# One list scheduler for all five engines up to block 8 of a chained attention and two-network kernel

## The chip, the cores and the metric

The kernel runs on one core of a Trainium2 chip. The metric is the device time of one execution in microseconds. The core has five engines that run side by side: TensorE (PE, with its weight loads as PEld), VectorE (DVE), ScalarE (ACT), GpSimd (POOL) and SyncE (SP), which here issues nearly all DMAs.

## The reference

All tensors are float32 except that the weights come as float64. Batch 8, 8 heads, 576 positions, head dimension 64; 4608 tokens of width 512 pass through both networks.

```
kv  = einsum('bhsd,bhse->bhde', k, v)
out = einsum('bhsd,bhde->bhse', q, kv)
x   = out / sqrt(mean(out * out, -1) + 1e-6) * g_norm      # to (4608, 512)
h   = max(x @ w1, x @ w2, x @ w3)                          # 512 -> 768
x   = h @ w_out                                            # 768 -> 512
r   = max(x @ w_in, 0)                                     # 512 -> 2048
out = (s * r * r + b) @ w_out2                             # 2048 -> 512
```

## The kernel before, in words

The tokens are cut into nine blocks of 512: blocks 0 to 7 are the first 512 positions of each batch element, block 8 is made of the 64 positions that are left of each of the eight (gathered in `o_rem`). A matrix product in full precision is three passes of PE (`mm3`, lines 95 to 98): each operand is split into a high part of the type fp32r and a low part, made by `split` (lines 91 to 93: ScalarE copies the high part, VectorE or GpSimd subtracts for the low one).

For each block `j` there is attention of batch element `bb` (block 0's own at the start, then that of block `j + 1` beside the products of block `j`), the first product (18 panels `g`, `g1_part`, line 352; `g1_out` takes the maximum of three panels on ScalarE and VectorE, lines 365 and 367) and the second (`g2_mm`, line 373). Attention of one element is four pairs `p` of heads: `load_kv`, `kv_mm` (line 236) into the bank `kvor`, a copy on ScalarE (`kv_out`, for element 0 `kv_diag_pair`, line 251), `q_turn` (line 266), `o_mm` (line 270), `o_out`, and then the norm of each pair: `o_sq`, `sq_split` (line 308), the mean square `ms_mm` into one bank `ms` (line 316; element 0 in the plain form of line 319, which is one matmul in f32, the others as two passes of fp32r), `ms_ln` (three ScalarE steps, lines 328 to 330), `ms_newton` (three VectorE steps, lines 336 to 338; the first is the last reader of `ms`) and `x_split`.

The weights arrive as float64 and are turned into float32 on the core: `conv_unpack` (lines 162 to 167: three ScalarE and three VectorE instructions), `conv_sum` (line 172, GpSimd) and `conv_split`. There are 18 panels for the first product and 6 blocks for the second, all needed within block 0, and three sets of buffers that hold a panel on its way (two while the six blocks are turned). The 32 pieces of the second network's weights are turned during the later blocks and put back to DRAM (`conv_store`).

After block 8 comes the second network (lines 508 on) in Strassen form, on which nothing changes.

What sets the order: each step is put into a list with a position (`at`), one place being one panel of a block (`SL` = 22 places a block; the start has its own scale `US`). `run` (line 68) issues the steps in the order of positions. Up to position 20 SP's queue keeps that order and the other engines are ordered by the framework; from there on PE and SP keep it, and VectorE, ScalarE and GpSimd are ordered by the framework.

## Time and profile before

| | us |
|---|---|
| median of 3 runs (1460.7 to 1464.87) | 1463.11 |
| the profiled execution, its time | 1459.22 |
| its span from the first to the last instruction | 1457.4 |
| PE busy | 1388.7 (95%) |
| VectorE busy | 914.0 (63%) |
| ScalarE busy | 785.8 (54%) |
| GpSimd busy | 319.6 (22%) |
| mean granted TensorE clock | 0.985 |

The shares are means over a span whose stages differ: the start up to about 151 us (block 0, all weights of the first network, attention of elements 0 and 1), blocks 1 to 7 up to 671 us, block 8 up to 736 us, and the second network to the end. The granted clock is a share of 2.4 GHz; half of it is 1.2 GHz. Spans of matmuls overlap, so a row that merges several gives the time that they took together.

### The profile page before, as it was taken

What the parts mean: (1) busy time and instruction counts of PE and PEld (TensorE: products, weight loads), DVE (VectorE), ACT (ScalarE), POOL (GpSimd) and SP (SyncE); (2) the same over time, 40 slices, a digit from 0 to 9 for tenths busy, and PEclk for the clock granted to TensorE, in tenths of its full rate; (3) what the DMA queues carried; (4) which work ended last, traced back from release to release, by engine and by line L of the source; (5) the groups of instructions that cost most, each with busy time, mean ns of one, the idle gap of its engine ahead of it and who ended that gap; (6) DMA issues with size and microseconds to landing.
All of it is one profiled execution on the core that took longest, in us unless ns stands there. A gap on an engine that the chain in (4) does not pass through costs nothing. (4 is left out here: it accounts for less than half of the span.)

```text
span 1457.4 us, 19593 instructions
## 1 busy us (share of the span) xinstructions
PE 1388.7 (95%) x6960; PEld 1127.0 (77%) x6960; DVE 914.0 (63%) x1418; ACT 785.8 (54%) x1389; POOL 319.6 (22%) x238
## 2 busy tenths in 40 slices
PE   5589999898999999999999999999999999999997
PEld 2367777787878787888878878878788888888887
DVE  4996344535353435355476765756777888888785
ACT  5774444435353434443365646646676666656565
POOL 1433232323132323321100000000002414141412
PEclk8789999999999999999999999999999999999999
DMA  9954606172362622213135464453677444454541
GB/s 231 245 167 62 135 22 159 54 158 78 110 125 80 148 87 59 78 31 116 58 130 200 162 230 176 143 202 121 215 261 239 130 151 169 154 170 149 179 135 40
DMA packets 229169, 202.61 MB, mean 139 GB/s; under 512 B 126032, under 2 KB 179280, under 8 KB 226896
## 3 DMA queue, kind: packets, MB, share of 16 engines
q1 hardware_dynamic: 228912, 201.11, 46.6%
q8 instruction: 54, 0.88, 0.3%
q14 instruction: 43, 0.35, 0.1%
q10 hardware_dynamic: 160, 0.26, 0.0%
HBM read 126.88 MB, written 74.45 MB: 138 GB/s over the span
## 5 line engine op out<-in xcount | busy, mean ns | idle before, releaser
L96 PE MATMUL g<-xh,w_w 128*128 128x512 f32 x648 | 258.4, 402 | 6.7 <-ACT xh L92 5.0
L97 PE MATMUL g<-xl,w_w 128*128 128x512 f32 x648 | 255.6, 394 | 0.1
L98 PE MATMUL g<-xh,w_w 128*128 128x512 f32 x648 | 255.1, 394 | 0.0
L92 ACT ACTIVATE zx<-z 128x512 fp32r<-128x512 f32 (+1 forms) x280 | 161.2, 586 | 123.2 <-PE zs_a L710 35.3
L632 PE MATMUL ps_a<-x_q,w_q 128*128 128x512 f32 (+1 forms) x960 | 211.2, 371 | 3.0 <-DVE cs L540 2.6
L710 PE MATMUL zs_a<-zx,w_q 128*128 128x512 f32 (+1 forms) x960 | 203.7, 369 | 0.5 <-POOL zx L93 0.3
L632 PEld LDWEIGHTS ps_a<-x_q,w_q 128*128 128x128 f32 x960 | 167.1, 188 | 38.6 <-DVE cs L540 5.8
L93 POOL TENSOR_TENSOR zx<-z,zx 128x512 fp32r<-128x512 f32 (+1 forms) x46 | 63.6, 1383 | 594.1 <-DMA gd<-cs 382.2
L93 DVE TENSOR_TENSOR zx<-z,zx 128x512 fp32r<-128x512 f32 (+1 forms) x234 | 171.9, 752 | 34.8 <-ACT zx L92 34.4
L710 PEld LDWEIGHTS zs_a<-zx,w_q 128*128 128x128 f32 x960 | 167.8, 188 | 31.9 <-POOL zx L93 0.7
L96 PEld LDWEIGHTS g<-xh,w_w 128*128 128x128 f32 x648 | 124.1, 192 | 37.8 <-ACT xh L92 6.6
L98 PEld LDWEIGHTS g<-xh,w_w 128*128 128x128 f32 x648 | 123.2, 190 | 26.4
L97 PEld LDWEIGHTS g<-xl,w_w 128*128 128x128 f32 x648 | 123.2, 190 | 26.3 <-POOL xl L93 0.8
L172 POOL TENSOR_TENSOR tr_ctr<-tr_ctr,gc_cgc 128x512 int32<-128x512 int32 x42 | 56.2, 1337 | 263.6 <-DVE gc_cgc L167 179.2
L162 DVE TENSOR_SCALAR gc_cgc<-raw_craw 128x512 uint16<-128x512 uint16 x42 | 19.9, 475 | 144.6 <-DMA raw_craw<-in_moe_w_in_dram 70.3
L632 PE MATMUL ps_b<-x_q,w_q 128*128 128x512 f32 (+1 forms) x480 | 107.6, 372 | 1.4 <-ACT cs L643 0.8
L710 PE MATMUL zs_b<-zx,w_q 128*128 128x512 f32 (+1 forms) x480 | 103.7, 370 | 2.1 <-DVE zx L93 2.1
L367 DVE TENSOR_TENSOR h<-g,h 128x512 f32<-128x512 f32 x108 | 73.8, 683 | 42.4 <-PE g L98 42.0
L632 PEld LDWEIGHTS ps_b<-x_q,w_q 128*128 128x128 f32 x480 | 83.8, 188 | 19.3 <-ACT cs L643 1.6
L710 PEld LDWEIGHTS zs_b<-zx,w_q 128*128 128x128 f32 x480 | 83.9, 188 | 18.9 <-DVE zx L93 3.3
L163 ACT ACTIVATE tr_ctr<-raw_craw 128x512 int32<-128x512 uint32 x42 | 28.0, 667 | 118.2 <-DMA wd<-tr_ctr 99.0
L96 PE MATMUL g<-h,w_o 128*128 128x512 f32 x216 | 84.1, 390 | 0.6 <-DVE h L367 0.6
(158 smaller groups left out, 2216.7 us busy)
## 6 DMA issues: line engine op xcount, KB each, us to landing
z<-gd SPq DMA_DIRECT2D x64, 512.0 KB
gd<-cs SPq DMA_DIRECT2D x96, 256.0 KB
z<-gd SPq DMA_DIRECT2D x48, 256.0 KB
x1d<-x SPq DMA_DIRECT2D x36, 256.0 KB
raw_craw<-in_moe_w_in_dram SPq DMA_DIRECT2D x16, 512.0 KB
wd<-tr_ctr SPq DMA_DIRECT2D x32, 256.0 KB
raw_craw<-in_moe_w_out_dram SPq DMA_DIRECT2D x64, 128.0 KB
gd<-d SPq DMA_DIRECT2D x32, 256.0 KB
```

What stands on the lines that cost most here:

```text
L92: act(out=hi, in_=src, func=AF.Copy)
L93: eng.tensor_tensor(out=lo, in0=src, in1=hi.bitcast(F32), op=ALU.subtract)
L96: nc.tensor.matmul(ps, lhsT=w[:, 0, sl], rhs=xh, start=first, stop=False)
L97: nc.tensor.matmul(ps, lhsT=w[:, 0, sl], rhs=xl, start=False, stop=False)
L98: nc.tensor.matmul(ps, lhsT=w[:, 1, sl], rhs=xh, start=False, stop=last)
L162: ts(out=c, in0=w16[:, :, 3], scalar1=0x7FFF, scalar2=None, op0=ALU.bitwise_and)
L163: act(out=r, in_=w32[:, :, 0], func=AF.Copy, scale=2.0 ** -29)
L172: nc.gpsimd.tensor_tensor(out=t, in0=t, in1=g.bitcast(I32), op=ALU.add)
L367: nc.vector.tensor_tensor(out=st["h", m], in0=ps, in1=st["h", m], op=ALU.max)
L632: nc.tensor.matmul(ps, lhsT=w[:, a, c], rhs=x[:, b_], start=new and k == 0 and e == 0, stop=k == HK - 1 and e == 2, skip_group_check=True)
L710: nc.tensor.matmul(ps, lhsT=w[:, a, c], rhs=x[:, b_, :n], start=new and k_ == 0 and e == 0, stop=k_ == 3 and e == 2, skip_group_check=True)
```

## The change

Every step up to position `CUT` (just ahead of block 8) becomes a `job` with its engine, a duration in us, and the names that it reads (`r`), writes (`w`) and allocates (`a`). `arrange` builds the dependences from these names and from the number of buffers of each tag (`SIZE`), and then plays the engines in time: whenever an engine is free it takes, of the jobs that are ready, the one with the lowest position. A VectorE job that begins while a GpSimd job runs is charged 0.9 us more; a job of SP is followed by 2.0 us until its data are there. The jobs are issued in the order of their begin, and within that region all five engines keep that order. Jobs from `CUT` on join the list of before.

The steps that held several instructions are cut into jobs of one each (`conv_unpack` becomes `conv_c`, `conv_r`, `conv_t`, `conv_m`, `conv_g`; `ms_ln` becomes `rsqrt`, `ms_newton` becomes `newton`, each split a high and a low job). Positions at the start are new. Element 0 goes through the same `kvc` and `rps` tiles as the others (`kvf` and its copies of half a diagonal go), all four pairs of its keys and values have `k` and `v` tiles (two had tiles of the tag `o`), and element 1 takes its mean squares in the plain form too (`PLAIN = 2`). In blocks 0 and 1's input the low parts are made by VectorE (before: two of four pairs of each by GpSimd). For elements 2 to 7 the keys and values of the pairs are loaded 3 places apart from 16 places ahead of the block (before: from 5.9 places ahead and 1 apart for elements 4 to 7, earlier for 2 and 3).

The core of the diff:

```diff
-    plan = []
+    plan, jobs = [], []
+    SIZE = {"g": 4, "t": 2, "st": 2, "qt": 2, "o": 2, "kvc": 3, "k": NP, "v": NP}
     def at(pos, fn, *args):
         plan.append((pos, len(plan), fn, args))
+    def job(pos, eng, cost, fn, *args, r=(), w=(), a=()):
+        jobs.append((pos, len(jobs), eng, cost, fn, args, r, w, a))
+    def arrange(todo):
+        writer, readers, users, owner, rings, need, after = {}, {}, {}, {}, {}, [], [[] for _ in todo]
+        for n, e in enumerate(todo):
+            owner.update((nm, n) for _, nm in e[8])
+            for nm in {key.split(":")[0] for key in (*e[6], *e[7])} | {nm for _, nm in e[8]}:
+                users.setdefault(nm, []).append(n)
+        for n, (_, _, eng, cost, fn, args, r, w, a) in enumerate(todo):
+            deps = set()
+            for tag, nm in a:
+                past = rings.setdefault(tag, [])
+                if past:
+                    deps.add((past[-1][0], False))
+                if len(past) >= SIZE.get(tag, 1):
+                    deps.update((m, True) for m in users[past[-SIZE.get(tag, 1)][1]])
+                past.append((n, nm))
+            for key in (*r, *w):
+                if key in writer:
+                    deps.add((writer[key], True))
+                if owner.get(key.split(":")[0], n) != n:
+                    deps.add((owner[key.split(":")[0]], False))
+            for key in w:
+                deps.update((m, True) for m in readers.pop(key, ()))
+                writer[key] = n
+            for key in r:
+                readers.setdefault(key, []).append(n)
+            deps = {d for d in deps if d[0] != n}
+            need.append(len(deps))
+            for m, full in deps:
+                after[m].append((n, full))
+        free, ready, heaps, out, pool = {}, [0.0] * len(todo), {}, [], 0.0
+        for n, e in enumerate(todo):
+            if not need[n]:
+                heaps.setdefault(e[2], []).append(n)
+        while any(heaps.values()):
+            begin, eng = min((max(free.get(e, 0.0), min(ready[n] for n in h)), e) for e, h in heaps.items() if h)
+            n = min(m for m in heaps[eng] if ready[m] <= begin)
+            heaps[eng].remove(n)
+            cost = todo[n][3]
+            if eng == "DVE" and begin < pool:
+                cost += 0.9
+            free[eng] = begin + cost
+            if eng == "POOL":
+                pool = begin + cost
+            end = begin + cost + (2.0 if eng == "SP" else 0.1)
+            out.append((begin, n))
+            for m, full in after[n]:
+                ready[m] = max(ready[m], end if full else begin)
+                need[m] -= 1
+                if not need[m]:
+                    heaps.setdefault(todo[m][2], []).append(m)
+        assert len(out) == len(todo)
+        return [todo[n] for _, n in out]
     def run():
-        todo = sorted(plan, key=lambda e: e[:2])
-        n = sum(e[0] < 20 for e in todo)
-        with tc.manual_schedule(engines={EngineType.SP}):
-            for _, _, fn, args in todo[:n]:
-                fn(*args)
+        order = sorted(jobs, key=lambda e: e[:2])
+        n = sum(e[0] < CUT for e in order)
+        with tc.manual_schedule(engines={EngineType.PE, EngineType.SP, EngineType.DVE, EngineType.Activation, EngineType.Pool}):
+            for e in arrange(order[:n]):
+                e[4](*e[5])
+        todo = sorted(plan + [(e[0], e[1] - len(jobs), e[4], e[5]) for e in order[n:]], key=lambda e: e[:2])
         with tc.manual_schedule(engines={EngineType.PE, EngineType.SP}):
-            for _, _, fn, args in todo[n:]:
+            for _, _, fn, args in todo:
                 fn(*args)
...
     def load_kv(bb, p):
-        kv = None if bb or p < 2 else at_.tile([P, 2, 2, C, D], F32, tag="o", bufs=NP // 2, name=f"kv_{p}")
-        for i, (nm, src) in enumerate((("k", k), ("v", v))):
-            t = st[nm, bb, p] = (at_.tile([P, 2, C, D], F32, tag=nm, bufs=NP, name=f"{nm}_{bb}_{p}")
-                                 if kv is None else kv[:, i])
+        for nm, src in (("k", k), ("v", v)):
+            t = st[nm, bb, p] = at_.tile([P, 2, C, D], F32, tag=nm, bufs=NP, name=f"{nm}_{bb}_{p}")
...
     def ms_mm(bb, p):
         ps = st["ms", p] = psa.tile([P, N], F32, tag="ms", name=f"ms_{bb}_{p}")
-        if bb == 0:
+        if bb < PLAIN:
             nc.tensor.matmul(ps, lhsT=onesf, rhs=st["sq", p], start=True, stop=True)
             return
...
+    def plan_conv(kk, src, pos, load, a, pr, gc, slot=None, store=None):
+        key = (kk[0], int(kk[1:]))
+        raw, tr, g = f"raw_{kk}", f"tr_{kk}", f"gc_{kk}"
+        c = g + "c:c" if gc == "st" else g + ":c"
+        ra, tra, gca = stage(a, pr, gc)
+        job(load, "SP", 2.23, conv_load, key, src, ra, w=[raw], a=[(a, raw)])
+        job(pos, "DVE", 0.43, conv_c, key, gca, r=[raw], w=[c], a=[(gc, g)] + ([(gc, g + "c")] if gc == "st" else []))
+        job(pos, "ACT", 0.67, conv_r, key, tra, r=[raw], w=[tr + ":r"], a=[(pr, tr)])
+        for i in range(2):
+            job(pos, "ACT", 0.71, conv_t, key, i, r=[c], w=[tr + ":t"])
+        job(pos, "DVE", 0.69, conv_m, key, r=[raw], w=[tr + ":r"])
+        job(pos, "DVE", 0.69, conv_g, key, r=[raw, tr + ":r"], w=[g + ":g"])
+        job(pos, "POOL", 1.35, conv_sum, key, r=[g + ":g"], w=[tr + ":t"])
+        if slot:
+            job(pos, "ACT", 0.63, conv_hi, key, slot, r=[tr + ":t"], w=[f"W_{kk}:0"], a=[(slot, f"W_{kk}")])
+            job(pos, "DVE", 0.69, conv_lo, key, r=[tr + ":t", f"W_{kk}:0"], w=[f"W_{kk}:1"])
+        else:
+            job(store, "SP", 1.1, conv_store, key, r=[tr + ":t"])
+    def plan_kv(bb, load, mm, n):
+        job(load(0) + 0.01, "SP", 1.1, load_rem, bb, w=["rem"])
         for p in range(NP):
...
+            job(load(p), "SP", 2.5, load_kv, bb, p, w=[f"k{bb}.{p}", f"v{bb}.{p}"],
+                a=[("k", f"k{bb}.{p}"), ("v", f"v{bb}.{p}")])
+            job(mm(p), "PE", 0.65, kv_mm, bb, p, r=[f"k{bb}.{p}", f"v{bb}.{p}", "rem"], w=[f"kvp:{p}"])
+        for p in range(0, NP, n):
+            job(mm(p + n - 1) + 0.01, "ACT", 0.4, kv_out, bb, p, n, r=[f"kvp:{i}" for i in range(p, p + n)],
+                w=[f"kvc{bb}:{i}" for i in range(p, p + n)], a=[("kvc", f"kvc{bb}")] if p == 0 else [])
...
+        job(t, "ACT", 0.59, square, r=r, w=[sq], a=[("sq", sq)])
+        if bb >= PLAIN:
+            job(t + u, "DVE", 0.42, sq_hi, bb, p, r=[sq], w=["h" + sq], a=[("sqh", "h" + sq)])
+            job(t + 1.2 * u, "POOL", 1.3, sq_lo, bb, p, r=[sq, "h" + sq], w=["l" + sq], a=[("sql", "l" + sq)])
+        job(t + 3.3 * u, "PE", 0.9 if bb < PLAIN else 0.46, ms_mm, bb, p, w=[ms], a=[("ms", ms)],
+            r=[sq] if bb < PLAIN else ["h" + sq, "l" + sq])
+        for n in range(3):
+            job(t + (4 + 0.3 * n) * u, "ACT", 0.65, rsqrt, bb, p, n, r=[(ms, y, y)[n]], w=[(y, y, uu)[n]],
+                a=[[("y", y)], [], [("u", uu)]][n])
+        for n in range(3):
+            job(t + (6 + 0.3 * n) * u, "DVE", 0.7, newton, bb, p, n, r=[[ms], [y], [uu, "g_sb"]][n], w=[[uu], [uu], o][n])
+        job(x, "ACT", 0.63, x_hi, bb, p, r=o, w=[f"xh{bb}:{p}"], a=[("xh", f"xh{bb}"), ("xl", f"xl{bb}")] if p == 0 else [])
+        job(x + 0.01, eng, 1.35 if eng == "POOL" else 0.69, x_lo, bb, p, nc.gpsimd if eng == "POOL" else nc.vector,
+            r=[*o, f"xh{bb}:{p}"], w=[f"xl{bb}:{p}"])
...
+    PLAIN = 2
+    CUT = SL * B - 0.2
+    Z = -12
     for p in range(NP):
...
+        plan_q(0, p, 1, Z + 0.2 + p)
+    plan_kv(0, lambda p: Z + p, lambda p: Z + p + 0.5, 1)
+    job(Z + 2.45, "SP", 1.0, load_scalars, w=["scalars"])
+    job(Z + 2.45, "DVE", 0.15, scale_g, r=["scalars"], w=["g_sb"])
     for p in range(NP):
...
+        plan_o(0, p // 2, [p], lambda p: Z + p + 0.4, Z + p + 0.6)
         if p % 2:
...
+            plan_oout(0, p // 2, Z + p + 0.7)
+        c = Z + p // 2 * 2 + 1.8 + 0.5 * (p % 2)
+        plan_norm(0, p, c, 0.1, c + 0.8, "DVE")
         for g in range(4):
...
+            plan_g1(0, g, Z + 7 + p + 0.01 * g, [p])
+    plan_rems(0, -1)
+    sets = [("craw", "ctr", "cgc"), tuple(WOS[3:]), tuple(WOS[:3])]
+    for n in range(G1):
+        plan_conv(f"w{n}", w1_src(n), 0.85 * n - 3 if n > 3 else Z + 3 + n, 0.85 * n - 5 if n > 3 else Z + 1.35 + n, *sets[n % 3], slot=W1S[n])
+    sets = [sets[0], (HS[M1 - 1], HS[M1 - 2], "st")]
+    for m in range(M1):
+        plan_conv(f"o{m}", [(0, P, wo[m * P:(m + 1) * P, :])], 12 + 0.8 * m, 10 + 0.8 * m,
+                  *sets[m % 2 if m < M1 - 1 else 0], slot=WOS[m])
...
+                plan_kv(bb, lambda p: -2 + p, lambda p: p + 0.5, NP)
             else:
...
+                plan_kv(bb, lambda p: t - 16 + 3 * p, lambda p: t - 0.8 + 0.001 * p, NP)
+            plan_q(bb, 0, NP, max(t - 10, 1))
+            for u in range(NP // 2):
+                a = t + (6 if bb > 1 else 6) * u + (4 if bb == 1 else 0)
+                plan_o(bb, u, [2 * u, 2 * u + 1], lambda p: a + 0.4 + 1.3 * (p % 2), a + 3)
+                plan_oout(bb, u, a + 3.7)
+                for i in range(2):
+                    p = 2 * u + i
+                    c, d = a + 3.9 + 2.9 * i, 0.9 if bb > 1 else 0.4
+                    plan_norm(bb, p, c, d, max(t + G1 + 0.2 + 0.5 * p, c + 7 * d), "POOL" if p < 3 and j else "DVE")
+            plan_rems(bb, t + 13.3)
...
```

## Rows read from the trace of the kernel before

**Rows 1.** The page's second part: busy tenths of TensorE in 40 slices.

```profile
...
PE   5589999898999999999999999999999999999997
...
```

**Rows 2.** The windows by block: stretch, length, busy us of each engine, clock, DMA.

```profile
...
0.00:39.06 39.06, 20.61 (x157) 10.58 (x157) 20.40 (x39) 24.05 (x43) 9.49 (x13) 0.86 0.99 236
39.06:84.77 45.71, 27.29 (x194) 17.93 (x193) 42.24 (x59) 34.84 (x61) 18.87 (x14) 0.80 0.83 213
84.77:133.74 48.97, 47.54 (x268) 36.98 (x269) 42.55 (x65) 32.31 (x56) 17.97 (x12) 0.95 0.66 138
133.74:150.99 17.25, 16.64 (x74) 13.40 (x72) 6.49 (x8) 5.17 (x9) 3.00 (x2) 1.00 0.02 8
150.99:223.13 72.14, 70.59 (x330) 56.28 (x328) 30.91 (x49) 30.63 (x51) 20.93 (x16) 1.00 0.36 86
223.13:301.26 78.13, 74.41 (x409) 59.71 (x408) 34.89 (x53) 32.93 (x54) 22.38 (x17) 0.98 0.44 115
301.26:380.13 78.87, 74.83 (x413) 59.75 (x409) 33.38 (x51) 32.17 (x54) 22.46 (x17) 0.98 0.44 103
380.13:455.53 75.40, 73.22 (x413) 58.61 (x409) 36.08 (x52) 33.02 (x54) 23.04 (x17) 1.00 0.50 113
...
530.93:603.78 72.85, 70.71 (x332) 56.34 (x329) 34.26 (x51) 33.19 (x55) 24.07 (x18) 1.00 0.24 66
603.78:670.98 67.20, 67.20 (x297) 55.56 (x296) 27.32 (x38) 26.08 (x43) 18.76 (x14) 1.00 0.21 59
670.98:736.27 65.29, 65.29 (x290) 54.05 (x288) 40.99 (x63) 28.55 (x50) 7.21 (x5) 1.00 0.27 94
...
```

**Rows 3.** The timeline of PE up to 151 us: start, length, engine, line, operation.

```profile
...
18.28 1.12 PE L245 MATMUL kvor<-kv 128*64 128x64 f32 x16
...
21.01 2.08 PE L319 MATMUL ms<-sq,onesf 128*128 128x512 f32 x2 [0.98 <-ACT sq L299]
...
74.68 1.82 PE L96 MATMUL g<-xh,w_w 128*128 128x512 f32 x4
...
84.77 0.80 PE L96 MATMUL g<-xh,w_w 128*128 128x512 f32 x1 [0.61 <-ACT h L365]
...
```

**Rows 4.** The waits from 151 to 671 us: total us, times, longest.

```profile
...
PE ms L322 <- DVE u L336: 14.7, 7, 3.7
...
```

**Rows 5.** The timeline of VectorE up to 151 us.

```profile
...
9.94 0.43 DVE L162 TENSOR_SCALAR gc_cgc<-raw_craw 128x512 uint16<-128x512 uint16 x1 [0.52 <-DMA raw_craw<-in_moe_w_dram]
...
28.48 0.43 DVE L162 TENSOR_SCALAR gc_cgc<-raw_craw 128x512 uint16<-128x512 uint16 x1 [3.88 <-DMA raw_craw<-in_moe_w_dram]
28.82 0.68 DVE L93 TENSOR_TENSOR w_w<-tr_o,w_w 128x512 fp32r<-128x512 f32 x1
29.42 0.68 DVE L336 SCALAR_TENSOR_TENSOR u<-ms,u 128x512 f32<-128x512 f32 x1
...
69.89 1.75 DVE L166 SCALAR_TENSOR_TENSOR tr_ctr<-raw_craw,tr_ctr 128x512 int32<-128x512 uint16 x1
...
140.82 0.68 DVE L93 TENSOR_TENSOR h<-h,h 128x512 fp32r<-128x512 f32 x1
```

**Rows 6.** Groups of GpSimd's instructions up to 151 us: busy us, mean ns.

```profile
...
L93 POOL TENSOR_TENSOR xl<-o,xh 128x512 fp32r<-128x512 f32 x4 | 6.0, 1520 | 4.0 <-ACT xh L92 4.0
L313 POOL TENSOR_TENSOR sql<-sq,sqh 128x512 fp32r<-128x512 f32 x4 | 5.8, 1440 | 10.1 <-DVE sqh L312 10.1
...
```

**Rows 7.** Groups of VectorE's instructions up to 151 us.

```profile
...
L167 DVE SCALAR_TENSOR_TENSOR gc_o<-raw_o,tr_o 128x512 uint32<-128x512 uint32 x12 | 9.2, 770 | 0.1
...
L367 DVE TENSOR_TENSOR h<-g,h 128x512 f32<-128x512 f32 x12 | 8.1, 676 | 0.0
...
```

**Rows 8.** The timeline of SP's queue: start, time that the issues take.

```profile
...
7.25 3.50 SPq L264 DMA_DIRECT2D qraw<-in_q_dram  x4
...
17.81 3.10 SPq L264 DMA_DIRECT2D qraw<-in_q_dram  x4
...
```

**Rows 9.** Groups of ScalarE's instructions up to 151 us.

```profile
...
L328 ACT ACTIVATE y<-ms,eps 128x512 f32<-128x512 f32 x8 | 5.5, 682 | 0.1
...
```

More of the change, by code (lines that the diff above doesn't have):

```diff
@@ new lines, in plan_q, with plan_o @@
+    def plan_q(bb, p, n, pos):
+        job(pos, "SP", 1.26 * n, load_q, bb, p, n, w=[f"qraw{bb}:{i}" for i in range(p, p + n)],
+            a=[("qraw", f"qraw{bb}")] if p == 0 else [])
+    def plan_o(bb, u, pp, turn, mm):
+        for p in pp:
+            job(turn(p), "DVE", 0.78, q_turn, bb, p, r=[f"qraw{bb}:{p}"], w=[f"qt{bb}.{p}"], a=[("qt", f"qt{bb}.{p}")])
+        job(mm, "PE", 0.7 + 0.5 * len(pp), o_mm, bb, u, pp, r=[x for p in pp for x in (f"qt{bb}.{p}", f"kvc{bb}:{p}")],
+            w=[f"ops{bb}.{u}:{p}" for p in pp] + [f"rps{bb}.{u}:{p}" for p in pp] + [f"kr:{2 * u}.{p}" for p in pp],
+            a=[("ops", f"ops{bb}.{u}"), ("g", f"rps{bb}.{u}")] if pp[0] == 2 * u else [])
@@ new lines, in plan_oout, with plan_rems, plan_norm, square @@
+    def plan_oout(bb, u, pos):
+        full = [f"ops{bb}.{u}:{p}" for p in (2 * u, 2 * u + 1)]
+        job(pos, "ACT", 1.02, o_out, bb, u, r=full, w=[f"o{bb}.{u}:0", f"o{bb}.{u}:1"], a=[("o", f"o{bb}.{u}")])
+        job(pos, "DVE", 0.2, o_rem_out, bb, u, r=[f"rps{bb}.{u}:{p}" for p in (2 * u, 2 * u + 1)], w=[f"or{2 * u + 1}:{bb}"])
+    def plan_rems(bb, pos):
+        job(pos, "DVE", 0.3, o_rems, bb, r=[f"kr:{c}.{p}" for c in (0, 2) for p in (c, c + 1)], w=[f"or0:{bb}", f"or2:{bb}"])
+    def plan_norm(bb, p, t, u, x, eng):
+        sq, ms, y, uu = (f"{c}{bb}.{p}" for c in ("sq", "ms", "y", "u"))
+        if bb < B:
+            o = [f"o{bb}.{p // 2}:{p % 2}"]
+            src = lambda: st["ops", p // 2][:, p % 2]
+            r = [f"ops{bb}.{p // 2}:{i}" for i in (p // 2 * 2, p // 2 * 2 + 1)]
+        else:
+            o = r = [f"or{p}:{b_}" for b_ in range(B)]
+            src = lambda: o_rem[:, p, :]
+        def square():
+            if bb == B:
+                st["o", B, p] = o_rem[:, p, :]
+            o_sq(bb, p, src())
+        job(t, "ACT", 0.59, square, r=r, w=[sq], a=[("sq", sq)])
[12 more added lines that the diff above has]
+            r=[*o, f"xh{bb}:{p}"], w=[f"xl{bb}:{p}"])
@@ L481, in attention_max_ffn_relu2_ffn @@
         for g in range(G1):
             if j or g >= 4:
[L483 to L486 removed]
+                plan_g1(j, g, t + g, range(KD))
+            plan_g1_out(j, g, t + max(g, j == 0 and 3 or 0) + 1.01)
         for n in range(KD):
```

259 lines of the change are left out of this document (108 added, 151 removed).

## The prediction

> **What bounds the kernel now.** I read the page's slices first, for the stretches where TensorE is not busy, then cut the span at the borders of the blocks. In the slices [rows 1] the row of PE is low only in the first three of 40 and in the last. The windows [rows 2] say the same by block. A block of the first network that carries no attention takes 65.29 us with PE busy all the time (670.98 to 736.27): the floor for a block. From 736 us on the change moves nothing. So all that can be won lies in two places.
>
> The first is the start. The second block's first matrix product begins at 150.99 us. Up to 39.06 us PE is busy half the time at a mean granted clock of 0.86, up to 84.77 us 60% of it at 0.80. VectorE is the engine that is full: 42.24 of 45.71 us in the second stretch, 42.55 of 48.97 us in the third. The DMA engines are full in the first (share 0.99) and at 0.83 in the second. The fourth input chunk of block 0 reaches PE at 74.68 us and panel 4 of the weights at 84.77 us [rows 3]; from there PE is 97% busy until 133.74 us. So the start has three limits in turn: DMA, VectorE, and a PE that got its work late.
>
> The second is the seven blocks from 150.99 to 670.98 us. Their idle PE time, stretch less busy, is 1.55 + 3.72 + 4.04 + 2.18 + 2.18 + 2.14 + 0 = 15.8 us (the stretch from 455.53 equals the one before it, so one stands). The stretches at 223 and 301 us are granted 0.98, and PE is busy 74.41 and 74.83 us there where the same work takes 73.22 us at 380 us: 2.8 us more. The waits name nearly all of the idle time: seven waits of the norm's mean-square product for VectorE's first Newton step, 14.7 us together [rows 4]. The only bank `ms` comes free with that step, which stood late in VectorE's order.
>
> **The change, the start.** What a panel needs on VectorE stays (L162, L166, L167, L93). Block 1 now takes its mean squares in the plain form, as block 0 did, so its four `sqh` and four `sql` go; the four `xl` that GpSimd made in the two blocks move to VectorE. VectorE back to back takes an instruction of 0.68 us every 0.60 us: the starts at 28.82 and 29.42 [rows 5]. It gains 4 x 0.60 us of `xl` and loses four shorter `sqh`: between 0 and +2.4 us, I take +1.
>
> GpSimd loses eight instructions (6.0 + 5.8 us) [rows 6]. What these took from VectorE I cost from both sides. A VectorE instruction that reads two operands from SBUF takes 1.75 us in place of 0.68 us when it meets a GpSimd one [rows 5], so eight fewer give back between 0 and 8 x 1.07 = 8.6 us. The mean of L167, 770 ns, says that not each GpSimd instruction meets one [rows 7]; I take 4 us. VectorE's sum to the end of block 0 is now 20.40 + 42.24 + 42.55 + 6.49 = 111.7 us [rows 2]; it becomes 108.7 us.
>
> When can that be done? VectorE waits for weights until 28.48 us [rows 5], behind q, k and v: a head pair of q alone keeps SP 3.1 to 3.5 us [rows 8]. The changed order puts k, v and q of pair 1 ahead of the first panel, which then is there at about 14 us in place of 9.94 us [rows 5]. I leave 28 us as the end of this phase, with some 9 us of VectorE work behind it. The remaining 99.7 us take 108 us at the fill of the second stretch (92%) and 103 us at 97%: VectorE is through at 131 to 136 us, against 141.5 us now (the last of [rows 5]).
>
> What is late next is the second product of block 0. Now it runs from 133.74 to 150.99 us in one piece, because PE had 14 panels to do after 84.77 us. With block 0's attention first in every engine's order the last chunk is there not at 74.68 us but at about 50 us: the last q is issued by 21 us in either kernel [rows 8], then come four norms in a row of about 6.5 us each (the product, 2.08 us for a pair of passes [rows 3], three ScalarE steps of some 0.7 us [rows 9], one Newton step until the bank is free, and half an instruction of waiting at each), then 3 us. From 50 us on PE follows the panels and the second product follows the last weight blocks, so only some 2 to 4 us of it lie behind VectorE's end. Block 1 starts at 133 to 140 us in place of 150.99 us; I take 136 us, **15 us less**, with bounds of 5 us (VectorE no fuller than now, the product's tail as hidden as said) and 24 us (VectorE at 100% from 28 us, and all 8.6 us back).
>
> Keys and values: the pairs of block 0 have tiles of their own now, so the ten DMAs of block 1's pairs wait on SP for block 0's products, and weight panels queue behind them. The DMA share of 0.99 says that they could not land sooner: I cost it at nothing. If the weights then come later, VectorE's largest wait for one, 3.88 us [rows 5], is what another would cost; if in an emptier stretch, that wait is what is won. For the later blocks the loads stand 3 places apart and up to 10 places earlier, with stores and conversions behind them on SP; the DMA share there is 0.21 to 0.50 [rows 2], so nothing. The half-diagonal copies on ScalarE become copies of a pair, under 1 us either way.
>
> **The seven blocks.** One list now orders all engines, so the mean-square product is put where the bank should be free. At best 15.8 us of idle time and 2.8 us of clock go: 18.6 us. The list's durations are not quite the chip's: it charges 0.69 us for VectorE's 0.60, and adds 0.9 us to any VectorE instruction that starts beside GpSimd. I keep 32 waits of 0.25 us, an estimate between none and the 2.1 us that each of the seven costs now: 18.6 - 8 = **11 us less**, bounds 0 and 18. The conversions of the second network have a low place but go as soon as an engine is free, so they come earlier; VectorE is at 31 to 36 of 72 to 79 us in these blocks [rows 2], which hides them.
>
> A rule of the Trainium skill bears on that 0.9 us (SBUF — State Buffer, section Who interferes with whom): a VectorE instruction with two SBUF operands contends with a GpSimd one that reads SBUF, the later one waiting for the other's end, while one with a single SBUF operand doesn't contend. The rows agree for both forms: 1.75 against 0.68 us [rows 5], and 676 ns on average for L367, whose other operand is in PSUM [rows 7]. By it the flat 0.9 us is wrong for L367 and the first Newton step. It moves places in the list, which the 8 us above covers; the sum by the one and by the other is the same.
>
> Sum against the profiled execution (span 1457.4, time 1459.2 us): 1459.2 - 15 - 11 = 1433 us. The median of the runs, 1463.1 us, is 3.9 us above that execution, so I forecast 1437 us, with 1422 to 1455 us as the forecast's own range.
>
> **The rivals.** (a) *Fixed queues wait on a cold PE: slower.* The list charges 0.65 us for a pair's key and value product and 0.9 us for a mean square, but the first 16 of that product's 20 matmuls take 1.12 us and a mean square 2.08 us at the low clock [rows 3]. In each of eight norms ScalarE and VectorE, whose order is now fixed, would sit through 1 to 2 us with conversions queued behind, 8 to 16 us at the engine that is the bound; with as much again for the products of keys and queries the 15 us are gone and 9 us more. The same in the seven blocks, 32 waits of 0.75 us, is 24 us against the 18.6 us: 5 us more. 1463 + 9 + 5 = 1477 us. It decides once VectorE's fill from 28 us to its end falls below about 80% and PE's waits for `ms` pass 19 us. Against it: both engines are faster than charged, which gives time back. (b) *VectorE is the bound whatever the order:* the start gives 5 us, the blocks 5 us: 1453 us. For it: it is 92% busy in the second stretch already. (c) *The full sum:* 24 + 18 us, and a few products of keys and values (2.5 us a block, 73.22 against 70.71 us [rows 2]) moved into PE's early gaps: 1463 - 45 = 1418 us. For it: all of that idle time has a name. (d) *The order made is near that of before:* 1463 us. The waits of 2 us at one and the same place in the blocks speak against it.
>
> **How the numbers follow.** Forecast 0.50, (c) 0.18, (b) 0.14, (a) 0.12, (d) 0.06. The likeliest gives 1437 us. The range takes in (b), (d) and most of (c) and leaves out (a) and the far end of (c): 1412 to 1463 us. What a measurement can tell from no change is 0.3%, so faster is below 1458.7 us: 0.81; same 0.08; slower 0.11.
>
> **What would show it.** Right: block 0's last chunk at PE before 60 us; block 1's first product at 133 to 140 us; VectorE above 92% busy from 30 us to 125 us; the seven blocks in at most 510 us in place of 520.0 us; a second network as long as before (721.1 us from 736.27 us to the end). Wrong: ScalarE or VectorE with gaps in the first 60 us that end with a PE product; PE's waits for `ms` still above 10 us; or a second network of another length, which the sum has at no change.

## The result, and the profile after

The changed kernel takes 1424.4 us (median of 1421.0 to 1427.0) against 1463.1 us: 0.9735 of the time before, with a 95% interval of 0.971 to 0.976. It is 38.7 us faster where 26 us were forecast; 1437 us missed by 12.6 us, inside the range. The profiled execution of the changed kernel took 1427.0 us, 2.6 us above its median, with a span of 1425.2 us. That of before was 3.9 us below its median. So the two traces account for 32.2 us, and the other 6.5 us lie between the executions that were profiled and the medians. One execution among the experiments, the profiled one of the first run without the middle part of the weights, ran at a mean granted clock of 0.655 and took 1960 us; it is left out of that run's time.

The page's slice row of the changed kernel, busy tenths of TensorE. After the third slice nothing but the last is below 9, where [rows 1] has two more slices of 8, and the two slices that were 5 and 5 are now 5 and 7:

```profile
...
PE   5789999999999999999999999999999999999997
...
```

The windows of the changed kernel, cut where its own stages end (columns as in [rows 2]):

```profile
...
0.00:24.84 24.84, 11.85 (x109) 6.38 (x109) 9.89 (x23) 11.61 (x21) 2.68 (x7) 1.00 0.98 210
24.84:80.00 55.16, 44.46 (x266) 30.36 (x267) 49.10 (x72) 39.76 (x68) 17.79 (x12) 0.85 0.91 232
80.00:120.40 40.40, 35.20 (x262) 25.92 (x260) 33.86 (x53) 31.66 (x55) 11.32 (x9) 0.92 0.96 222
120.40:141.27 20.87, 20.38 (x137) 15.58 (x135) 17.90 (x28) 12.72 (x22) 3.87 (x3) 1.00 0.51 164
141.27:211.37 70.10, 70.10 (x333) 56.55 (x330) 39.09 (x57) 34.89 (x59) 24.96 (x18) 1.00 0.51 119
...
281.33:353.86 72.53, 72.53 (x409) 58.66 (x408) 41.65 (x58) 37.36 (x61) 27.52 (x20) 1.00 0.52 109
...
636.49:701.77 65.28, 65.28 (x289) 54.07 (x288) 32.75 (x51) 25.80 (x45) 7.46 (x5) 1.00 0.15 59
701.77:1425.20 723.43, 708.51 (x3401) 590.39 (x3399) 531.37 (x844) 440.91 (x811) 108.24 (x78) 1.00 0.49 168
...
141.27:636.49 495.22, 495.22 (x2509) 401.35 (x2506) 238.52 (x356) 221.84 (x367) 161.64 (x116) 1.00 0.41 95
...
0.00:141.27 141.27, 111.88 (x768) 78.24 (x769) 110.74 (x173) 95.74 (x164) 35.66 (x30) 0.92 0.87 215
...
```

Read against [rows 2] by stage: the start ends at 141.27 in place of 150.99 us (-9.7). The seven blocks take 495.22 in place of 520.0 us (-24.8), and PE has no idle time in them. Block 8, the floor of the prediction, takes 65.28 against 65.29 us, and the second network 723.4 against 721.1 us (+2.3). The four make -32.2 us. The second network's 2.3 us are no more than executions differ by: a later one of the same kernel had 719.9 us there.

**The seven blocks.** The idle time of [rows 2], 15.8 us, is gone whole. PE's busy time fell by another 9.0 us, from 504.2 to 495.2 us. One part of that is a product of keys and values that moved: 400 matmuls of such products now lie ahead of block 1, before it was 320. One element has 80 of them (four pairs of 20), so these are five elements against four. A block with one and a block without differ by 72.53 - 70.10 = 2.4 us. Another part is the clock. These windows of the kernel before surround three of its waits for the mean-square bank:

```profile
...
262.00:266.10 4.10, 0.38 (x3) 0.01 (x1) 2.52 (x5) 2.88 (x5) 1.16 (x2) 1.00 0.35 123
266.10:270.00 3.90, 3.90 (x12) 3.04 (x12) 3.20 (x4) 1.67 (x3) 2.01 (x2) 0.64 0.02 6
345.00:349.00 4.00, 4.00 (x11) 3.19 (x12) 2.30 (x4) 1.94 (x4) 1.26 (x2) 0.59 0.00 0
497.40:500.00 2.60, 2.60 (x12) 2.15 (x13) 1.86 (x3) 0.24 (x1) 0.00 (x0) 1.00 0.76 151
...
```

After the waits of 3.7 and 3.2 us the products ran partly at the lower level, 0.64 and 0.59 of the clock on average, though PE was busy throughout; after the wait of 2.2 us at 497 us the clock stayed at 1.00. That is 3.90 x 0.36 + 4.00 x 0.41 = 3.0 us lost, or a little more, since the first of them had not ended at 270 us. The remaining 3.6 us are spread: a block of the same content at full clock is 0.5 to 0.7 us shorter (72.53 against 73.22, 70.10 against 70.71 us). Most of it lies at the edges of the waits, which the busy time counts in. Here is one wait of the kernel before:

```profile
...
494.81 0.39 PE L98 MATMUL g<-xh,w_w 128*128 128x512 f32 x1
497.37 0.50 PE L322 MATMUL ms<-sqh,ones 128*128 128x512 f32 x1 [2.17 <-DVE u L336]
497.71 0.39 PE L323 MATMUL ms<-sql,ones 128*128 128x512 f32 x1
...
```

In a dense stretch a matmul starts every 0.23 us (the next two here at 497.94 and 498.17 us) and the tail of its 0.39 us is covered by the next. The last one ahead of a wait shows its whole 0.39 us, and the first one behind it keeps the next 0.34 us away: 0.16 + 0.11 = 0.27 us for a wait, an estimate from these starts. For the nine waits that the trace of before names (the seven of [rows 4], one of 0.6 and one of 0.4 us) that makes about 2.4 of the 3.6 us. The rest was not traced.

**The start.** PE's busy time ahead of block 1 is the same, 111.88 us against 112.1 us in [rows 2], now with one more element's product of keys and values in it. The timeline of PE in the changed kernel (start, length, operation, and in brackets the wait ahead of it):

```profile
...
4.58 1.12 PE L319 MATMUL kvor<-v,k 128*64 128x64 f32 x16 [4.58 <-DMA v<-in_v_dram]
...
48.24 0.50 PE L155 MATMUL g<-xl,w_w 128*128 128x512 f32 x1 [0.52 <-DVE xl L267]
...
64.44 0.33 PE L319 MATMUL kvor<-vrem,krem 128*64 128x64 f32 x4 [3.28 <-DMA vrem<-in_v_dram]
...
67.97 1.12 PE L319 MATMUL kvor<-v,k 128*64 128x64 f32 x16 [3.19 <-DMA v<-in_v_dram]
...
97.61 0.48 PE L319 MATMUL kvor<-vrem,krem 128*64 128x64 f32 x4 [3.92 <-DMA vrem<-in_v_dram]
...
```

The last chunk of block 0 (its low part) reaches PE at 48.24 us, where [rows 3] has the chunk at 74.68 us. But PE stops three times for keys and values of elements 2 and 3. Its waits up to 141.3 us (total us, times, longest):

```profile
...
PE kvor L319 <- DMA v<-in_v_dram: 8.3, 4, 4.6
PE kvor L319 <- DMA vrem<-in_v_dram: 8.1, 4, 3.9
...
```

Of these 16.4 us, 5.5 are element 0's own (4.58 us of them the wait for the first load of all). The other 11 us, of PE's 29.4 idle us of the start, are for later elements, and 6.8 of them lie where the clock is low (0.85 from 24.84 to 80 us). At the end of the start two engines stand in line behind PE. The timeline of ScalarE and VectorE there:

```profile
...
134.99 0.69 DVE L267 TENSOR_TENSOR w_o<-tr_ctr,w_o 128x512 fp32r<-128x512 f32 x1
...
138.59 0.60 ACT L461 ACTIVATE x<-g 128x512 f32<-128x512 f32 x1 [3.64 <-PE g L156]
...
139.64 0.62 ACT L264 ACTIVATE xh<-o 128x512 fp32r<-128x512 f32 x1
...
140.29 0.69 DVE L267 TENSOR_TENSOR xl<-o,xh 128x512 fp32r<-128x512 f32 x1 [1.69 <-ACT xh L264]
...
```

ScalarE's copy of a finished second product waits 3.64 us for PE. The `xh` that block 1 needs stands behind it, then `xl` on VectorE, which ends at 140.98 us. That chain cost nothing here, since PE had work until 141.27 us. Block 0's second product ran from 120.40 to 141.27 us with PE busy for 20.38 of these 20.87 us. VectorE's last part of a weight block (`w_o` above) was done at 135.68 us, 5.6 us ahead of block 1: at the end PE itself was late.

### The profile page after: what moved, and what is told of

Same layout as the page of the kernel before. It is cut to its first block, busy times and chain, and to the rows that moved or that the text cites. A ratio compares the mean times of both kernels' runs of the same rounds, so it can differ in the third digit from the quotient of the medians.

```text
span 1425.2 us, 19581 instructions
## 1 busy us (share of the span) xinstructions
PE 1380.9 (97%) x6960; PEld 1124.0 (79%) x6960; DVE 913.4 (64%) x1420; ACT 784.3 (55%) x1385; POOL 313.0 (22%) x229
## 5 line engine op out<-in xcount | busy, mean ns | idle before, releaser
L154 PEld LDWEIGHTS g<-xh,w_w 128*128 128x128 f32 x648 | 122.1, 188 | 30.3 <-ACT xh L264 2.6
L156 PEld LDWEIGHTS g<-xh,w_w 128*128 128x128 f32 x648 | 122.1, 188 | 28.3 <-DVE w_w L267 2.6
L267 POOL TENSOR_TENSOR h<-h,h 128x512 fp32r<-128x512 f32 x40 | 55.3, 1382 | 225.1 <-ACT h L264 225.1
L762 PEld LDWEIGHTS ps_b<-x_q,w_q 128*128 128x128 f32 x480 | 83.9, 188 | 18.9 <-ACT cs L773 2.0
L840 PEld LDWEIGHTS zs_b<-zx,w_q 128*128 128x128 f32 x480 | 83.9, 188 | 18.9 <-DVE zx L151 3.3
L264 ACT ACTIVATE h<-h 128x512 fp32r<-128x512 f32 x54 | 34.0, 629 | 103.9 <-DVE h L442 103.4
```

The costliest lines, as they stand in the source:

```text
L154: nc.tensor.matmul(ps, lhsT=w[:, 0, sl], rhs=xh, start=first, stop=False)
L156: nc.tensor.matmul(ps, lhsT=w[:, 1, sl], rhs=xh, start=False, stop=last)
L264: act(out=out, in_=src, func=AF.Copy)
L267: eng.tensor_tensor(out=out, in0=src, in1=hi.bitcast(F32), op=ALU.subtract)
L762: nc.tensor.matmul(ps, lhsT=w[:, a, c], rhs=x[:, b_], start=new and k == 0 and e == 0, stop=k == HK - 1 and e == 2, skip_group_check=True)
L840: nc.tensor.matmul(ps, lhsT=w[:, a, c], rhs=x[:, b_, :n], start=new and k_ == 0 and e == 0, stop=k_ == 3 and e == 2, skip_group_check=True)
```

## The experiments

The questions, in order: is it the list or the new places; do the early loads cost PE its time; is VectorE or PE the bound of the start; do the list's wrong durations cost anything. "Block 1" below is the start of that block's first product in the profiled execution. Each window row of the start ends there.

### The list only up to block 1

```
-    CUT = SL * B - 0.2
+    CUT = SL - 0.2
```

> The changed kernel with the list scheduler ending at position 21.8 in place of 175.8: block 0 and the weights are still ordered by it, blocks 1 to 7 go by positions on PE and SP and by the framework on the other engines, as in the kernel before. Theory 1 (the order of the five engines is what took the waits of PE for the bank ms out of the seven blocks): those come back, 13 us of waits or more in the seven blocks, the blocks 15 to 22 us longer than the 495.2 us of the changed kernel, the time 1439 to 1447 us, the start unchanged at 141 us within 2. Rival 1 (the seven blocks gained because keys, values and the second network's weights are loaded and made at other times, not by order): the blocks stay within 5 us of 495.2, the time at most 1430 us.

Measured: 1456.5 us, 0.9973 [0.9951, 0.9995] of before. Its windows and the waits in the seven blocks:

```profile
...
139.89:669.21 529.32, 510.38 (x2666) 407.69 (x2665) 226.70 (x347) 220.81 (x366) 154.38 (x116) 0.99 0.40 97
...
```

```profile
...
PE ms L389 <- DVE u L405: 18.5, 10, 3.3
...
```

Expected were 15 to 22 us more in the blocks, and 1439 to 1447 us. The start is as good as with the whole list (139.89 us), with two elements' products of keys and values fewer in it (240 matmuls). The blocks take 34.1 us more than after: 18.9 us idle, nearly all of it the wait for the mean-square bank of [rows 4], and 15.2 us more busy. About 5 us of that are the two elements' products; the rest is slower or longer products. That the list's order made the gain in the blocks is shown; its size was underrated again. The rival, other load times, is out too: in the third experiment below three elements' loads move out of the start, and PE still has no idle time in the blocks. One rival was not run: the same steps fixed on all five engines in order of their places. Here VectorE, ScalarE and GpSimd went back to the framework's order, so the runs don't separate the simulated times from the mere fixing of all queues.

### No list at all

```
-    CUT = SL * B - 0.2
+    CUT = -100
```

> The changed kernel without the list scheduler (CUT at -100): its steps, tiles and places are kept, PE and SP go by places from the first instruction on, the other engines by the framework. Theory L (the list made from durations, not the new steps and places, brings the start's gain): block 1 begins at 148 us or later, the blocks take about the 529 us of e1_block0_only, the time is 1462 to 1480 us. Rival (new places, plain mean squares, tiles of their own): block 1 begins at 143 us or earlier, the time is 1453 to 1460 us.

Measured: 1469.8 us, 1.0065 [1.0044, 1.0087]: 0.65% slower than before. The profiled execution took 1463.7 us, the fastest of the four.

```profile
...
0.00:142.77 142.77, 104.98 (x609) 73.53 (x609) 107.49 (x171) 94.90 (x162) 37.22 (x30) 0.84 0.73 167
142.77:673.43 530.66, 510.50 (x2669) 408.77 (x2665) 225.75 (x346) 219.84 (x366) 154.05 (x116) 0.99 0.40 96
...
```

```profile
...
PE ms L389 <- DVE u L405: 20.0, 10, 4.3
...
```

Here the expectation split. The time came out as the theory said that the list makes the gain, the start as its rival said: the changed steps and places alone bring block 1 from 150.99 to 142.77 us. Of these 8.2 us, 2.5 are a product of keys and values fewer in the start (240 matmuls, three elements). The list brings it to 141.27 us with two elements' products more, 5 us of PE's work. How the start's gain divides depends on what such a product is worth there. At 2.5 us each the places and steps bring 8.2 - 2.5 = 5.7 us and the list 1.5 + 5 = 6.5 us. At the 1.1 us each that the next experiment shows (3.4 us for three) it is 7.1 and 3.7 us. So places and steps do about half or more in the start. In the blocks all of the gain is the list's, and the new steps and places without it are worse than the old order (530.66 against 520.0 us, 2.5 us of it the product).

### Later keys and values held back

```
-  job(load(p), "SP", 2.5, load_kv, bb, p, w=[...])
+  job(load(p), "SP", 2.5, load_kv, bb, p, r=["W_o5:1"] if bb > 1 else [], w=[...])
```

The remainders likewise, and no load of a later element has a place below 20.

> The changed kernel, with the keys and values of elements 2 to 7 held back until the last weight block of the first network is turned. Theory A (in the start these loads keep the DMA engines at 0.91 to 0.96, weight panels come late behind them, and PE in its fixed order stands 3.28, 3.19 and 3.92 us in front of their products): block 1 begins 7 to 11 us earlier, at 130 to 134 us, and one product more of 2.5 us stands in the blocks, so 5 to 8 us less in all, 1416 to 1420 us. Theory B (VectorE is the bound of the start, 110.7 us of work by 141 us): block 1 begins at 141 us within 3, the time is 1424 to 1430 us.

Measured: 1428.7 us, 0.9771 [0.9752, 0.979].

```profile
...
0.00:137.88 137.88, 106.29 (x529) 70.45 (x529) 109.09 (x170) 94.77 (x161) 38.37 (x30) 0.89 0.70 163
137.88:641.45 503.57, 503.57 (x2745) 408.15 (x2744) 237.78 (x359) 223.82 (x370) 162.20 (x116) 1.00 0.44 109
...
```

```profile
...
PE ops L351 <- DVE qt L338: 14.8, 4, 4.7
...
```

Block 1 comes 3.4 us earlier, not 7 to 11, nor within the 3 us of the other theory, whose range for the time was met; the DMA share falls from 0.87 to 0.70, and PE waits for the turned queries (2.4 us with the whole change) in place of keys and values. The blocks take 8.4 us more, as three elements' products have moved there. So holding these loads back gains the start less than the theory said, with new waits in place of the old, and loading early is worth 5 us net (503.57 - 495.22 - 3.39). What the start would be without either wait this run can't tell.

### Less VectorE work in the start

For panels with their own slot the reading of the middle part of the weights is left out, twice the same kernel:

```
-        job(pos, "DVE", 0.69, conv_m, key, r=[raw], w=[tr + ":r"])
+        if not slot:
+            job(pos, "DVE", 0.69, conv_m, key, r=[raw], w=[tr + ":r"])
```

> The changed kernel without the VectorE instruction that adds the middle 16 bits of each weight (conv_m), for the 24 panels and blocks of the first network: their weights lose these bits. 24 x 0.60 = 14.4 us of VectorE's work in the start go, nothing else. Theory B (VectorE bounds the start): block 1 begins 9 to 14 us earlier, at 127 to 132 us, the time 1410 to 1416 us. Theory A (DMA and the products behind the early loads): at most 4 us earlier, 1420 us or more.

The first gave 1419.6 us (three executions), 0.9712 [0.9687, 0.9737], but no trace at full clock:

> The kernel of e3_no_mid again (the middle 16 bits of the first network's weights left out, 14.4 us of VectorE's work less in the start), for a profile at full clock. Its time came out 3 us under the changed kernel's, not 9 to 14. Theory P (PE is the bound of the start's second half: 111.9 us busy up to 141 us at a mean clock of 0.92, with the products of keys and values of five elements in it and 10 us of waits for their loads): VectorE shows 12 us or more of new idle time before block 1, PE's idle time stays above 20 us, block 1 begins at 136 to 141 us. Theory B (VectorE): block 1 begins before 132 us and the time was a matter of the second network.

Measured: 1420.5 us, 0.9736 [0.9698, 0.9774].

```profile
...
0.00:131.93 131.93, 108.29 (x649) 75.39 (x650) 93.46 (x150) 94.30 (x163) 35.90 (x30) 0.92 0.85 206
131.93:631.25 499.32, 499.32 (x2625) 404.62 (x2624) 235.37 (x354) 222.15 (x368) 161.60 (x116) 1.00 0.42 100
...
```

17.3 us less on VectorE (93.46 against 110.74) bring block 1 9.3 us earlier, just inside the 132 us of the theory that VectorE bounds the start; the 136 to 141 us of the theory that PE does is missed. But of the 9.3 us the blocks give back 4.1, since only 280 matmuls of keys and values lie in the start, 120 fewer, and PE too has 3.6 us less to do there. Net that is 5.2 us, and the times of 1419.6 and 1420.5 us miss the 1410 to 1416 us that the theory gave.

### Less PE work in the start

Block 0's products leave out the pass with the low part of the weights:

```
-        nc.tensor.matmul(ps, lhsT=w[:, 0, sl], rhs=xl, start=False, stop=False)
+        nc.tensor.matmul(ps, lhsT=w[:, 0, sl], rhs=xl, start=False, stop=last and j == 0)
+        if j == 0:
+            return
```

> The changed kernel without the third pass (low part of the weight by high part of the input) of both products of block 0 alone: 96 of 288 matmuls, 96 x 0.227 = 21.8 us of PE's work at full clock in the start; the order of all engines is kept. Theory P (PE bounds the second half of the start): block 1 begins 8 to 18 us earlier, before 133 us, the time 1406 to 1416 us. Theory B (VectorE bounds it): at most 4 us earlier, 1420 us or more.

Measured: 1416.3 us, 0.9712 [0.9682, 0.9743].

```profile
...
0.00:131.22 131.22, 89.14 (x672) 59.08 (x673) 107.12 (x170) 94.23 (x162) 36.45 (x30) 0.92 0.94 229
131.22:626.47 495.25, 495.25 (x2508) 401.25 (x2505) 238.26 (x359) 223.72 (x369) 161.65 (x116) 1.00 0.40 96
...
```

22.7 us less on PE (89.14 against 111.88) bring block 1 10.1 us earlier, within the 8 to 18 us that the theory of PE as the bound said, with the same 400 matmuls of keys and values in the start. The time is 0.3 us above its range. With the run before it: PE relieved gives 10.1 of 22.7 us, VectorE relieved 9.3 of 17.3 us, or 5.2 us without what the blocks give back. The start has no single bound; PE and VectorE hold it together.

### Slow-clock durations for PE

```
-  job(mm(p), "PE", 0.65, kv_mm, ...)
+  job(mm(p), "PE", 1.55 if bb < 2 else 0.65, kv_mm, ...)
-  job(t + 3.3 * u, "PE", 0.9 if bb < PLAIN else 0.46, ms_mm, ...)
+  job(t + 3.3 * u, "PE", 2.05 if bb == 0 else 0.9 if bb < PLAIN else 0.46, ms_mm, ...)
```

In the same way 2.45 us for block 0's attention products, and 1.3 in place of 0.68 us a chunk for the first four panels.

> The changed kernel, with the durations that the list charges for PE's steps of attention 0 and of panels 0 to 3 raised to what the rows at the low clock show (key and value product 1.55 for 0.65 us, query product 2.45 for 1.2, mean square of element 0 2.05 for 0.9, a quarter panel 1.3 for 0.68). Only the order can change. Theory C (ScalarE and VectorE stand in fixed order in front of a PE that is slower than charged: ScalarE 3.05, VectorE 1.64 and 1.83 us up to 36 us): block 1 begins 3 to 8 us earlier, 1416 to 1421 us. Theory B: within 3 us of 141 us, 1421 to 1428 us.

Measured: 1420.7 us, 0.9719 [0.9697, 0.974], block 1 at 135.83 us. Beside the changed kernel once more:

> The changed kernel once more, on the same chip as the next one, so that the two can be compared: block 1 at 141.3 us within 1, 1421 to 1426 us.

> The kernel of e4_cold_pe once more. Its profile had block 1 5.4 us earlier than the changed kernel's; its time stood only 2 us lower, within the interval. If the order made with PE's durations at the low clock is better by itself (theory C), block 1 begins at 135.8 us within 1.5 again and the time is 3 us or more below e11_changed_again. If the 5.4 us were of that one execution, less than 2 us.

Measured: 1423.2 us (1422.0 to 1424.8), block 1 at 139.75 us, for the changed kernel; 1418.6 us (1417.6 to 1421.9), block 1 at 136.30 us, with the slow-clock durations. The difference is 4.65 us, and no run of the one reaches into those of the other, though the nearest two, 1421.92 and 1421.97 us, almost touch. The changed kernel's block 1 came 1.5 us earlier than in its first trace, more than the 1 us expected; differences of that size in the start, as the 1.5 us above for the list, say little. The windows of the start of the first run with the slow-clock durations, and of the seven blocks of the second:

```profile
...
24.84:80.00 55.16, 46.34 (x287) 32.40 (x287) 51.54 (x80) 45.50 (x77) 17.59 (x12) 0.97 0.96 252
...
0.00:135.83 135.83, 110.84 (x768) 77.54 (x768) 109.12 (x173) 96.36 (x164) 36.34 (x30) 0.97 0.90 224
...
```

```profile
...
136.30:631.51 495.21, 495.21 (x2508) 401.32 (x2505) 241.09 (x356) 221.63 (x367) 161.06 (x116) 1.00 0.41 95
...
```

From 24.84 to 80 us PE, VectorE and ScalarE all do more in the same time (VectorE 51.54 against 49.10 us, ScalarE 45.50 against 39.76 us), and the clock there is 0.97 in place of 0.85 (0.94 and 0.81 in the second executions). The blocks are unchanged. The waits of the start name two things that went. These are of the changed kernel:

```profile
...
ACT o L361 <- PE ops L351: 7.5, 3, 3.1
...
DVE o_rem L370 <- PE rps L357: 3.8, 2, 2.1
...
```

and these of the first run with the slow-clock durations:

```profile
...
PE kvor L319 <- DMA vrem<-in_v_dram: 5.2, 3, 3.3
PE kvor L319 <- DMA v<-in_v_dram: 4.9, 2, 4.7
...
ACT o L361 <- PE ops L351: 1.0, 1, 1.0
...
```

ScalarE's waits for PE's query product fall from 7.5 to 1.0 us (up to 40 us from 4.9 to none), and VectorE's of 3.8 us are gone: this is the mechanism of rival (a), fixed queues waiting on a slow PE. PE's own waits for keys and values fall in the same order from 16.4 to 10.1 us. The two are not separated. Together they cost the changed kernel 3.5 to 5.4 us, all of it in the start. At 0.9713 [0.9694, 0.9732] of the time before, this is the lowest time here of a version that does the whole computation.

The Trainium skill (TensorE: Matmul & The Clock Gate, section "Part 1: The HAM clock gate (the "warmup" mystery)") puts the cost of the slow phase below 1% of a typical span and advises models not to fit a particular count of slow products. The size agrees: the start's mean clock of 0.92 can cost at most 0.08 x 141 = 11 us, 0.8% of the time (an estimate). But where the model is what orders the engines, charging some products as slow was worth 4.65 us, 0.3%.

### Loads charged with a longer way

The durations as in the last, and every load charged as landing 6 us after its issue:

```
-            end = begin + cost + (2.0 if eng == "SP" else 0.1)
+            end = begin + cost + (6.0 if eng == "SP" else 0.1)
```

> The kernel of e4_cold_pe, in which the list besides counts on data 6.0 us after a load's slot on SP in place of 2.0. Only the order can change. Theory A' (PE stands in fixed order in front of loads that the list takes to be there: 3.28, 3.19 and 3.92 us): PE's waits for k, v and their rests up to 141 us, 8.1 us for the rests alone, fall below 4 us, and block 1 begins 3 to 7 us before the 135.8 us of e4_cold_pe; 1413 to 1418 us. Rival (another limit takes their place): 135.8 us within 2, 1419 to 1423 us.

Measured: 1423.2 us, 0.9756 [0.9729, 0.9784].

```profile
...
0.00:141.38 141.38, 115.30 (x828) 80.17 (x829) 107.98 (x171) 96.26 (x163) 38.05 (x30) 0.92 0.89 224
141.38:634.72 493.34, 493.34 (x2446) 399.41 (x2444) 234.43 (x356) 222.68 (x367) 161.24 (x116) 1.00 0.39 92
...
```

The waits for the remainders are 2.7 us, against 5.2 us with the slow-clock durations alone, but those for keys and values themselves rise from 4.9 to 7.4 us:

```profile
...
PE kvor L319 <- DMA v<-in_v_dram: 7.4, 3, 4.6
...
PE kvor L319 <- DMA vrem<-in_v_dram: 2.7, 2, 1.4
...
```

Their sum stays at 10.1 us, where less than 4 us was expected, and block 1 is 5.5 us later, which neither the theory nor its rival allowed. The intended saving did not come about, so the theory is not upheld. Of the 5.5 us, 1.1 are more idle time and 4.5 are more busy time of PE (115.30 against 110.84 us): 60 more matmuls of keys and values have come into the start, about 1.9 us at 2.5 us for 80, and the clock there is 0.92 in place of 0.97.

### Keys and values as close together as before

```
-                plan_kv(bb, lambda p: t - 16 + 3 * p, ...)
+                plan_kv(bb, lambda p: t - 5.9 + p, ...)
```

> The changed kernel with the keys and values of elements 2 to 7 placed as elements 4 to 7 were before: from 5.9 places ahead of the block, 1 apart, in place of 16 ahead and 3 apart. My sum had this part at nothing, since a queue that is free takes what is ready whatever its place: 1422 to 1427 us, block 1 at 141 us within 2. Rival (the place keeps loads of elements 3 to 5 out of the start): block 1 begins 3 us or more earlier and the blocks carry one or two products more, 2.5 us each, 1424 to 1430 us.

Measured: 1423.0 us, 0.9756 [0.973, 0.9782].

```profile
...
0.00:140.66 140.66, 109.09 (x768) 76.34 (x769) 109.68 (x173) 95.99 (x164) 35.80 (x30) 0.93 0.88 216
140.66:635.88 495.22, 495.22 (x2509) 401.33 (x2506) 239.59 (x356) 221.97 (x367) 162.02 (x116) 1.00 0.41 95
...
```

Nothing changes: "loaded further apart" is worth nothing under the list, as the sum had it.

### Truer durations for VectorE and ScalarE

The slow-clock durations, and for every VectorE and ScalarE step the distance between starts in place of its recorded length. The surcharge beside GpSimd is 1.07 us, and steps that read PSUM or turn the queries have none; a step's result counts as ready 0.15 us after its end in place of 0.1 (a few of the lines):

```
-            if eng == "DVE" and begin < pool:
-                cost += 0.9
+            if eng == "DVE" and begin < pool and not one:
+                cost += 1.07
-        job(pos, "DVE", 0.69, conv_g, ...)
+        job(pos, "DVE", 0.6, conv_g, ...)
```

> The kernel of e4_cold_pe, in which VectorE and ScalarE too are charged as the traces show them: 0.60 us from start to start for an instruction of 0.68 us (0.69 in the list), 0.52 to 0.62 for ScalarE's (0.63 to 0.71), and 1.07 us beside GpSimd for instructions with two operands in SBUF alone (0.9 for all). Only the order can change. Theory (the order is near its best, VectorE and PE both bound the start): block 1 begins at 135.8 us within 3 and the time is that of e12_cold_again within 3 us. Rival (wrong durations cost waits): block 1 begins 4 us or more before that.

Measured: 1429.5 us, 0.9781 [0.9761, 0.98].

```profile
...
0.00:135.63 135.63, 106.48 (x689) 75.36 (x690) 110.14 (x174) 96.36 (x165) 37.40 (x30) 0.94 0.86 211
135.63:637.49 501.86, 499.72 (x2585) 403.13 (x2584) 234.75 (x355) 218.27 (x366) 157.87 (x116) 1.00 0.40 97
...
```

```profile
...
PE ms L391 <- DVE u L407: 0.9, 1, 0.9
...
```

Block 1 comes when the theory said, but the time is 11 us above that of the same durations without this edit, where 3 us was expected. The start is as with the slow-clock durations, with one element's product less in it. The blocks take 6.6 us more: 2.1 us of waits, among them one for the mean-square bank, which had none, about 2.5 us for a product that moved back, and 2 us not traced. The rest lies behind block 7 (1.7 us) and between the profiled execution and the median (3.3 us). That a charge above the truth is slack for the bound engine is a reading of this one run. Since lengths, surcharge and the 0.15 us were changed together, which of them brought the waits back is open.

## Why the prediction came out as it did

**The bound and the two places: right.** All of the gain lies up to the end of block 7; the floor block is equal to 0.01 us, and the second network differs by less than two executions of one kernel do.

**The start, 15 us forecast, 9.7 us measured (11.2 us in the second execution): right in sign, too large.** The step on the last chunk held, 48.24 us for "about 50 us". VectorE's sum was near, 110.7 for 108.7 us. Two terms failed. One is VectorE's fill from 28 us to its end, 92 to 97% in the sum. The window of the changed kernel:

```profile
...
28.00:135.68 107.68, 91.57 (x601) 66.55 (x598) 94.14 (x140) 80.27 (x136) 32.18 (x23) 0.90 0.86 216
...
```

Its waits of the start name what it lacked:

```profile
...
DVE w_w L267 <- ACT w_w L264: 5.2, 6, 1.6
...
```

The fill was 87%, with waits for the high parts that ScalarE makes (5.2 us), for the loads of the second product's weights (4.0 us) and for PE. That VectorE was still done at 135.68 us, inside the forecast's 131 to 136 us, is luck: until then it had 94.1 us to do and not 99.7. The other term is the tail. I had 2 to 4 us of the second product behind VectorE's end; it was 5.6 us, all of it busy time of PE, which had three pairs of keys and values to multiply within the second product. Both have one root, which the experiments show from both sides (less VectorE work -9.3 us, less PE work -10.1 us): I made VectorE the one bound and let PE follow.

**The seven blocks, 11 us forecast, 24.8 us measured: right in mechanism, the largest miss.** The term that failed is the 8 us kept for 32 waits of 0.25 us; it measured 0, though the list's durations are as wrong as I said. I had counted their being wrong as a cost, and for the truer ones the waits came back (2.1 us). Beyond the 18.6 us that I called possible lay 2.5 us of a product that moved into the start, which I had put into rival (c) alone, and 3.6 us of shorter blocks, of which some 2.4 us are the edges of the waits: I had counted each wait at its idle time alone.

**Loads of keys and values at no cost: right for their spacing, not for their order.** The spacing is worth nothing. But with the queue free, the list takes what is ready, and five elements' products lie ahead of block 1. Three of them held back gave the start 3.4 us and cost the blocks 8.4 us.

**The median:** I added 3.9 us for the distance between the profiled execution and the median. After the change the profiled execution stood 2.6 us on the other side. 6.5 of the 12.6 us missed are this, the rest is +13.8 (blocks), -5.3 (start) and -2.3 us (second network).

**The rivals.** (a), fixed queues on a slow PE, is real in the start, within the 3.5 to 5.4 us of the slow-clock durations, and at nothing in the blocks. The sign that I gave for it, gaps in the first 60 us that end with a PE product, was there (4.9 us of ScalarE's waits and 5.6 us of VectorE's up to 40 us). Its point of decision, waits for `ms` above 19 us, was reached only without the list (20.0 us), and there the kernel was slower than before. (b), VectorE as the bound whatever the order, holds a part of the start. (c), the full sum at 1418 us, was right for the blocks; its start at -24 us was not. (d) is out.

**GpSimd beside VectorE:** the prediction's rule, that a VectorE instruction with a single operand in SBUF is not held up, is too wide. In the trace after, `conv_c` (L217), with one operand in SBUF, takes 0.42 us alone and 1.20 to 1.51 us in the four places where it begins while a GpSimd instruction runs (1.50 us at 46.08 us, beside one from 45.66 to 47.30 us). The list's flat surcharge is right for that step.

## What to carry to other kernels

Where engines that take their work in order are coupled through one or two buffers, the waits of the bound engine can be a matter of order and not of work: here an order made for all engines at once removed 15.8 us of waits and the clock that they had cost, while the same steps, with PE and SP sorted by place and the others left to the framework, had 18.9 us. In such an order charge the bound engine what it really takes, its slow clock too. That the others should be charged rather more than they take is suggested by one run. And when a filler is pulled into early gaps, look at what waits for the filler's data: 11 us of PE's waits in the start were for work that wasn't due, though pulling it in still paid.

## What the hardware showed that I had not expected

- A wait can cost more than its length: after waits of 3.7 and 3.2 us in the middle of dense work PE ran the next 4 us at 0.64 and 0.59 of the clock on average, after one of 2.2 us at 1.00.
- The second network, untouched, took 723.4 and 719.9 us in two executions of the same kernel; a change under 4 us can't be read from one execution's span.
